# Two bursts per pair instead of five short steps: reordering an attention stream inside a PE-bound kernel

## The chip, the core and the metric

The kernel runs on one core of one Trainium2 chip. The core has a matrix engine (PE, with its weight loads shown apart as PEld), a vector engine (DVE), a scalar engine (ACT), a general engine (POOL) and a queue engine that issues DMAs (SP). Each runs its own instructions strictly in the order in which the program lists them and waits at semaphores for the others. The metric is device time in microseconds (us). All times here are of one execution each; six executions of the kernel before were timed, and one more number, the span, comes from the profiled one.

## The reference, cut to what matters

```python
# q, k, v: (8 batches, 8 heads, 576 positions, 64), float32
scores = scale * q @ k.T
mask   = local (0 <= i-j < 32) for heads 0-3, strided (i >= j, i % 32 == j % 32) for heads 4-7
x      = softmax(where(mask, scores, -1e9)) @ v          # -> (4608 tokens, 512)
h      = x @ w_in                                        # (4608, 2048)
out    = relu(h)**2 @ w_out                              # (4608, 512)
```

## The kernel before

**Two streams on one PE.** The matrix part (MoE) is cut into 9 chunks of 512 tokens. For each chunk `mm1(c, ff)` (L402) makes 128 of the 2,048 hidden columns: four matmuls of 128x512 into one `ph` bank, a relu on ACT (L411, out `r`), and a square on DVE (L412, out `g_sb`). `mm2(c, i)` (L416) is a quarter of one output block: four matmuls of 128x512 (L423); after every fourth, ACT copies the block to `y` and SP writes it out. I call each such call a *group*; there are 288, numbered from 0. From chunk 3 on, `mm1` of chunk c and `mm2` of chunk c-1 alternate; before that they run in blocks (groups 32 to 47 are `mm1` of chunk 1, 48 to 63 `mm2` of chunk 1, 64 to 79 `mm1` of chunk 2).

**Attention is woven in between.** The unit is a pair of heads: pair u = 4 * batch + p, where p = 0, 1 are local and p = 2, 3 strided. After batch 0, which runs by itself ahead of the groups, each pair has these steps:

- T: PE transposes q and k (L233), with a copy on ACT (q) or DVE (k, L248). Only for the earlier batches; later ones have it done by DMA (L150, L162).
- S(u) (`step_S`, L254): 12 (local) or 16 (strided) small matmuls of 64 rows of contraction (L277) into four PSUM tiles `pt`. Four exps follow on ACT (L282) and two mask multiplies on DVE (L288), one for each head. They are not issued at once: the first exp comes with the step; `later(k, ...)` (L292 to L296) defers the second exp by one group, the first mask and the third exp by two, the fourth exp by three and the second mask by four. Each lands behind that group's relu or square in its engine's order.
- D(u, part) (`step_D`, L342): 6, 6 or 4 matmuls (L359) of the exps with v, then a reciprocal and a multiply on DVE (L370, L371), out `x_l` or `x_s`. A local pair has two parts, a strided pair three. Before its matmuls, a D step issues at once whatever of its own pair's deferred work is not issued yet (L343).
- E(u) (`step_E`, L374): the transpose of x into `xt`. Local pairs of batch 2 and later do it by one DMA from SP's queue (L381). Strided pairs use 8 transposes on PE (L388) and a copy (L396), on ACT for u < 12 and on DVE from there.

The scores, the D outputs and the transposes share one pool of five PSUM banks (`ps_t`); `r` has four buffers, `ph` two.

**What sets the order.** `stream_steps` (L459) lists the steps: for each u the order is S(u+1), E(u-1), D(u,0), [T], D(u,1), [T], and D(u,2) for a strided pair. `ends[u-1]` notes the place in this list at which E(u-1) is over. The planner at the end of the kernel then spreads the list over the groups: for each batch b it takes the steps between the last `ends` and `ends[4*b+3]` and assigns them in proportion to group weights, with one count for each step in the list, whatever it holds:

```python
for b in range(1, B):
    g_end, s_end = ready.get(b, starts[b]), ends[4 * b + 3]
    ...
    for g in range(g_prev, g_end + 1):
        due[g] = done_prev + (s_end - done_prev) * sum(weights[g_prev:g]) // total
```

The last E of batch b is thus due exactly ahead of the first `mm1` group that reads batch b: groups 80, 112, 144, 176 and 208 for batches 3 to 7 (batch 1 by group 32, batch 2 by group 56).

Of the kernel before, what the change touches and what calls it, by code (L numbers as in the profile page):

```python
# [14 lines left out]
def kernel(  # L15
# [78 lines left out]
    def is_local(u):  # L94
        return units[u][1] < H // 4
# [118 lines left out]
    def run_due(test):  # L214
        due = [x for x in pending if test(x)]
        for x in due:
            pending.remove(x)
        for x in sorted(due, key=lambda x: x[0]):
            x[2]()
# [5 lines left out]
    def step_T(u, name):  # L225
        s = st[u]
        local = is_local(u)
        n, w = (6, QL) if local else (NJ, SP_)
        src = s[name]
        src = src.rearrange("p j h d -> p (j h d)" if local else "p h c -> p (h c)")  # L230
        pt = ps_t.tile([128, S], BF16, name="pt")
        for j in range(n):
            nc.tensor.transpose(pt[:, w * j:w * (j + 1)], src[:, 128 * j:128 * (j + 1)],  # L233
                                ident[0:w, 0:w])
        if local and name == "k":
            full = kTl[v_slot(u)]
            dst = full[:, 32:32 + S]
        else:
            full = dst = qkT.tile([128, S], BF16, name=f"{name}T")
        if local:  # L240
            o = dst.rearrange("c (p j) -> c p j", j=6)
            i = pt.rearrange("c (j p) -> c p j", j=6)
        else:
            o, i = dst, pt
        if name == "q" and u not in (1, 3):
            nc.scalar.copy(o, i)
        else:
            nc.vector.tensor_copy(o, i)  # L248
        s[name + "T"] = full

    def blk_pos(h, j):
        return NJ * (j % 2) + 4 * h + j // 2
# [89 lines left out]
    def step_D(u, part):  # L342
        run_due(lambda x: x[1] == u)  # L343
        s = st[u]
        e, vt = s["e"], s["v"]
        if is_local(u):
            w, kn, n0, n1, tot = QL, 128, 6 * part, 6 * part + 6, 2 * NL
            rhs = vt.rearrange("p h t d -> p (h t) d")
            pos = lambda n: QL * n
            src = lambda n: n  # L350
        else:
            w, kn, tot = SP_, SP_, NBS
            n0, n1 = ((0, 6), (6, 12), (12, 16))[part]
            rhs = vt
            pos = lambda n: SP_ * blk_pos(n % 2, n // 2)
            src = lambda n: NJ * (n % 2) + n // 2
        po = ps_t.tile([128, 6, D + 1], FP32, name="pt")
        for n in range(n0, n1):
            nc.tensor.matmul(po[:, n - n0, :], e[0:kn, pos(n):pos(n) + 128],  # L359
                             rhs[0:kn, src(n), 0:D + 1], start=True, stop=True)  # L360
        if part == 0:
            s["x"] = x_pool.tile([w, tot, D], BF16, name="x_l" if is_local(u) else "x_s")
        x = s["x"]
        if is_local(u):
            x = x.rearrange("p (t h) d -> p h t d", h=2)[:, part]
        else:
            x = x[:, n0:n1, :]
        m = n1 - n0
        rinv = small.tile([128, 6, 1], FP32, name="rinv")
        nc.vector.reciprocal(rinv[0:w, 0:m], po[0:w, 0:m, D:D + 1])  # L370
        nc.vector.tensor_tensor(x, po[0:w, 0:m, 0:D],  # L371
                                rinv[0:w, 0:m].to_broadcast([w, m, D]), op=ALU.mult)

    def step_E(u):  # L374
        s = st[u]
        b, p = units[u]
        x = s["x"]
        local = is_local(u)
        n, w = (NL, QL) if local else (NJ, SP_)
        if local and b >= XB:  # L380
            nc.sync.dma_start_transpose(  # L381
                out=xt[p][:, b * S:(b + 1) * S].rearrange("c (t q) -> c t q", q=QL),
                in_=x.rearrange("p n d -> p (n d)"))
            st.pop(u)
            return
        px = ps_t.tile([128, S], BF16, name="pt")
        for t in range(n):
            nc.tensor.transpose(px[:, w * t:w * (t + 1)],  # L388
                                x[:, 2 * t:2 * t + 2, :].rearrange("p h d -> p (h d)"),
                                ident[0:w, 0:w])  # L390
        dst = xt[p][:, b * S:(b + 1) * S]
        copy = nc.scalar.copy if u < 12 else nc.vector.tensor_copy
        if local:
            copy(dst, px)
        else:
            copy(dst.rearrange("c (p j) -> c p j", j=NJ),  # L396
                                  px.rearrange("c (j p) -> c p j", j=NJ))
        st.pop(u)
# [32 lines left out]
    T_ = lambda u, nm: (lambda: step_T(u, nm))  # L431
    S_ = lambda u: (lambda: step_S(u))
    D_ = lambda u, part: (lambda: step_D(u, part))
    E_ = lambda u: (lambda: step_E(u))
# [9 lines left out]
    def first_steps():  # L444
        t, n, o = T_, (lambda u: lambda: step_N(u)), (lambda u: lambda: step_O(u))
        order = []
        for i, u in enumerate(first_order):
            order += [t(u, "q"), t(u, "k")]
            if i > 1:
                order.append(n(first_order[i - 2]))  # L450
            order.append(S_(u))
        a, b, c, d = first_order
        order += [n(c), lambda: run_due(lambda x: x[1] == d), o(a), n(d), o(b), o(c), o(d)]
        return [(fn, 0 if i < len(order) - 7 else 6) for i, fn in enumerate(order)]

    def has_T(u):
        return units[u][0] < (LB if is_local(u) else XB)

    def stream_steps(lo, hi, base):  # L459
        order = [T_(lo, "q"), T_(lo, "k"), T_(lo + 1, "q"), S_(lo), T_(lo + 1, "k")]  # L460
        ends = {}
        for u in range(lo, hi + 1):
            if u < hi - 1:
                order.append(S_(u + 1))
            if u > lo:
                order.append(E_(u - 1))
                ends[u - 1] = base + len(order)
            if u < hi:
                order.append(D_(u, 0))
                if u + 2 < hi and has_T(u + 2):  # L470
                    order.append(T_(u + 2, "q"))
                order.append(D_(u, 1))
                if u + 2 < hi and has_T(u + 2):
                    order.append(T_(u + 2, "k"))
                if not is_local(u):
                    order.append(D_(u, 2))
        return order, ends
# [65 lines left out]
    for e in es:  # L543
# [3 lines left out]
                            base=-1, channel_multiplier=1, pattern=[[-1, QL]])  # L547
    nc.gpsimd.affine_select(out=ml, in_=ml, compare_op=ALU.is_ge, fill=0.0,
                            base=32, channel_multiplier=-1, pattern=[[1, QL]])
# [7 lines left out]
                            base=0, channel_multiplier=-1, pattern=[[1, SP_]])  # L557
# [5 lines left out]
    first = first_steps()  # L563
# [9 lines left out]

    NCH = T // 512
    steps, ends = stream_steps(4, 8, 0)
    more, more_ends = stream_steps(8, 4 * B, len(steps))
    steps = steps + more
    ends.update(more_ends)
# [108 lines left out]
```

## Time and profile before

| | |
|---|---|
| six timed executions | median 325.72 us (323.76 to 327.46) |
| the profiled execution | 326.22 us, of which the profiled span is 324.2 us (2.0 us lie around it) |
| matmuls of 128x512 | 1,152 records (L408 576, L423 576), each shown as about 380 ns |
| mean start-to-start of those, within a group of four | 216 ns (for instance 102.442 to 102.658 us, and 103.026 to 103.241) |
| ACT busy, DVE busy | 164.4 us (51%), 168.6 us (52%) |
| granted PE clock | 1.00 in all stretches from 4 us to the end of the span |

The page gives busy time by engine, a row of tenths over the span, the chain that ended last, and groups of instructions with what ended the idle time before them. Matmuls are pipelined, so that their shown durations overlap: a group of four takes 0.86 us from its first start to the next group's first start, though its bar is 1.03 us long. Starts are what is compared below. In a timeline line the columns are start, length, engine, source line, operation, output<-inputs, shape and count; an idle gap ahead of it and what ended that gap follow in brackets.

### The profile page before, as it was taken

How to read it: one execution, taken by the hardware profiler on the slowest of the kernel's cores; microseconds unless marked ns; L12 is line 12 of the kernel's file. 1: busy time of each engine (PE TensorE's matmuls, PEld its weight loads, DVE VectorE, ACT ScalarE, POOL GpSimd, SP SyncE). 2: the span in 40 equal slices, each digit the busy share in tenths (PEclk: the TensorE clock that was granted, in tenths of full speed). 3: DMA queues.
4: the chain of work that ended last, by engine and by line, in shares of the span. 5: the costliest groups of instructions: out<-in, count | busy, mean ns of one | idle time of the engine just before them, and what ended most of it. 6: DMA issues, size and time to landing. Idle time of an engine off the chain costs nothing.

```text
span 324.2 us, 6229 instructions
## 1 busy us (share of the span) xinstructions
PE 304.3 (94%) x2390; PEld 153.1 (47%) x2390; DVE 168.6 (52%) x413; ACT 164.4 (51%) x338; POOL 87.2 (27%) x113
## 2 busy tenths in 40 slices
PE   2699999899989998999999999999999999999995
PEld 1465445444555544444444544454445444444442
DVE  5544555656975786656566656565455222222200
ACT  3662764567745674544554555554554444444411
POOL 8514472573920813722074007000000000000000
PEclk9999999999999999999999999999999999999999
DMA  7999999999999999999499557000110010000021
GB/s 182 182 195 229 208 151 253 195 291 232 214 140 201 208 223 180 216 192 188 111 212 228 137 123 172 34 32 34 51 53 32 32 67 33 32 34 32 32 95 69
DMA packets 87222, 44.81 MB, mean 138 GB/s; under 512 B 71769, under 2 KB 80377, under 8 KB 87001
## 3 DMA queue, kind: packets, MB, share of 16 engines
q1 hardware_dynamic: 77448, 34.81, 49.4%
q0 software_dynamic: 9744, 9.60, 18.6%
q8 instruction: 19, 0.31, 0.4%
q14 instruction: 11, 0.08, 0.1%
HBM read 36.89 MB, written 12.98 MB: 154 GB/s over the span
## 4 chain that ended last, share of the span: by engine, by line
PE 88%; DVE 5%; DMA 2%; ACT 2%; issue 1%; ACTq 0%; POOLq 0%
PE ph L408 38%; PE py L423 27%; PE ph L423 10%; PE pt L277 4%; PE pt L359 4%; DMA qT_s<-in_q_dram 2%; PE pt L233 2%; PE py L440 2%; DVE e L288 1%; DVE xt L396 1%; PE pt L388 1%; DVE x_s L371 1%; PE pt L332 1%; ACT e L282 1%; DVE kTl L248 1%
## 5 line engine op out<-in xcount | busy, mean ns | idle before, releaser
L408 PE MATMUL ph<-xt,w_in_b 128*128 128x512 bf16 x576 | 146.2, 382 | 1.8 <-DVE xt L396 1.7
L411 ACT ACTIVATE r<-ph 128x512 bf16<-128x512 f32 x144 | 86.0, 597 | 104.6 <-PE ph L408 99.5
L412 DVE TENSOR_TENSOR g_sb<-r 128x512 bf16<-128x512 bf16 x144 | 69.0, 480 | 107.1 <-ACT r L411 106.3
L423 PE MATMUL py<-w_out_b,g_sb 128*128 128x512 bf16 x400 | 102.7, 379 | 0.0
L423 PEld LDWEIGHTS <-g_sb 128*128 128x128 bf16 x576 | 52.8, 98 | 59.6 <-issue 3.1
L408 PEld LDWEIGHTS <-w_in_b 128*128 128x128 bf16 x576 | 52.2, 98 | 54.9 <-issue 2.0
L282 ACT ACTIVATE e<-pt 72x288 bf16<-72x288 f32 (+1 forms) x128 | 48.7, 406 | 14.4 <-PE pt L277 14.2
L423 PE MATMUL ph<-w_out_b,g_sb 128*128 128x512 bf16 x176 | 42.4, 379 | 0.0
L181 POOL CAST vl<-vl_st 128x768 bf16<-128x768 f32 x14 | 13.8, 984 | 57.4 <-DMA vl_st<-in_v_dram 41.4
L359 PEld LDWEIGHTS <-e 128*128 128x128 bf16 (+1 forms) x392 | 21.0, 97 | 15.6 <-DVE e L288 0.5
L288 DVE TENSOR_TENSOR e<-e,mask_str 72x576 bf16<-72x576 bf16 x32 | 19.2, 602 | 7.8 <-ACT e L282 7.8
L371 DVE TENSOR_TENSOR x_s<-pt,rinv 72x384 bf16<-72x384 f32 (+1 forms) x42 | 21.4, 509 | 1.4
L122 POOL CAST q_l<-q_st 96x768 bf16<-96x768 f32 x15 | 12.6, 839 | 26.4 <-DMA q_st<-in_q_dram 22.6
L427 ACT COPY y<-py 128x512 f32<-128x512 f32 x25 | 14.6, 585 | 4.0 <-PE py L423 4.0
L122 POOL CAST k_l<-k_st 96x768 bf16<-96x768 f32 x14 | 12.1, 863 | 16.9 <-DMA k_st<-in_k_dram 16.6
L370 DVE RECIPROCAL rinv<-pt 96x6 f32<-96x6 f32 (+2 forms) x70 | 12.9, 184 | 6.5 <-PE pt L359 6.5
L427 ACT COPY y<-ph 128x512 f32<-128x512 f32 x11 | 6.4, 585 | 19.4 <-PE ph L423 19.4
L371 DVE TENSOR_TENSOR x_l<-pt,rinv 96x384 bf16<-96x384 f32 x28 | 15.5, 554 | 1.0
L197 POOL CAST vs<-v_st 72x1024 bf16<-72x1024 f32 x14 | 15.4, 1126 | 0.5 <-DMA v_st<-in_v_dram 0.2
L288 DVE TENSOR_TENSOR e<-e,mask_loc 128x576 bf16<-128x576 bf16 x32 | 14.9, 464 | 1.0 <-ACT e L282 1.0
L359 PE MATMUL pt<-vs,e 72*128 72x65 bf16 x224 | 13.8, 193 | 0.1
L182 POOL CAST vl<-vl_st 32x640 bf16<-32x640 f32 x14 | 11.7, 835 | 0.9
(74 smaller groups left out, 156.2 us busy)
## 6 DMA issues: line engine op xcount, KB each, us to landing
out_dram<-y SPq DMA_DIRECT2D x36, 256.0 KB, 2.0
vl_st<-in_v_dram SPq DMA_DIRECT2D x28, 144.0 KB, 3.6
v_st<-in_v_dram SPq DMA_DIRECT2D x14, 288.0 KB
q_st<-in_q_dram SPq DMA_DIRECT2D x8, 288.0 KB, 7.7
k_st<-in_k_dram SPq DMA_DIRECT2D x8, 288.0 KB, 8.2
q_st<-in_q_dram SPq DMA_DIRECT2D x16, 144.0 KB, 7.9
k_st<-in_k_dram SPq DMA_DIRECT2D x16, 144.0 KB, 6.5
w_in_b<-in_moe_w_in_dram POOLq DMA_DIRECT2D x4, 512.0 KB, 11.2
```

The costliest lines, as they stand in the source:

```text
L122: copy(t.rearrange("p j h d -> p h j d"), s[name + "f"].rearrange("p h (j d) -> p h j d", j=6))
L181: nc.gpsimd.tensor_copy(t[:, :, :, 0:D].rearrange("p h t d -> p (h t) d"), s["vf"])
L197: (copy or nc.gpsimd.tensor_copy)(t[:, :, 0:D], s["vf"].rearrange("p h (j d) -> p (h j) d", d=D))
L282: nc.scalar.activation(e[0:kn, lo:lo + S // 2], banks[row][half][0:kn, 0:S // 2], AF.Exp, scale=scale)
L288: nc.vector.tensor_tensor(x, x, m.to_broadcast([kn, n, w]), op=ALU.mult)
L359: nc.tensor.matmul(po[:, n - n0, :], e[0:kn, pos(n):pos(n) + 128], rhs[0:kn, src(n), 0:D + 1], start=True, stop=True)
L371: nc.vector.tensor_tensor(x, po[0:w, 0:m, 0:D], rinv[0:w, 0:m].to_broadcast([w, m, D]), op=ALU.mult)
L408: nc.tensor.matmul(ph, w_in_b[:, kk, 128 * ff:128 * (ff + 1)], xt[kk][:, 512 * c:512 * (c + 1)], start=(kk == 0), stop=(kk == 3))
L411: nc.scalar.activation(r, ph, AF.Relu)
L412: later(1, lambda: nc.vector.tensor_tensor(g[:, ff, :], r, r, op=ALU.mult))
L423: nc.tensor.matmul(py, g[:, ff, 128 * j:128 * (j + 1)], w_out_b[:, ff, :], start=(ff == 0), stop=(ff == 15))
L427: nc.scalar.copy(y, py)
```

## The change

For u >= 12 (batch 3 on), `stream_steps` puts S(u+1) and E(u-1) into one list entry, and all D parts of pair u into another:

```diff
         for u in range(lo, hi + 1):
+            if u >= 12:
+                first = ([S_(u + 1)] if u < hi - 1 else []) + [E_(u - 1)]
+                order.append(lambda f=first: [fn() for fn in f])
+                ends[u - 1] = base + len(order)
+                if u < hi:
+                    order.append(lambda u=u: [step_D(u, i) for i in range(2 if is_local(u) else 3)])
+                    if u + 2 < hi and has_T(u + 2):
+                        order += [T_(u + 2, "q"), T_(u + 2, "k")]
+                continue
             if u < hi - 1:
                 order.append(S_(u + 1))
```

No instruction is added or dropped, and the order among the attention steps themselves stays S, E, D, D, D. A batch from 3 on has 8 entries in place of 18 (16 in batch 7, where no S of a next batch is left), so that in batches 4 to 7 an entry comes every fourth group. The entry counts also move steps of pairs below 12: S(13) with E(11), at u = 12, is one entry, which makes batch 2's stretch one entry shorter and shifts the proportional assignment there. In the two lists, the group ahead of which each step stands:

| step | before | after |
|---|---|---|
| S(8), S(9) | 37, 40 | 38, 40 |
| D(8,0), D(8,1) | 41, 42 | 41, 43 |
| D(9,0), D(9,1) | 46, 47 | 47, 48 |
| T(12) k, D(10,2), S(12) | 51, 52, 52 | 52, 52, 53 |
| E(10), D(11,0), D(11,1), D(11,2) | 53, 53, 54, 55 | 53, 54, 55, 56 |
| S(13) with E(11) | 56 | 56 |
| D(15,0), D(15,1), D(15,2) | 73, 75, 77 | 76 |
| S(17), E(15) | 79, 80 | 80 |
| D(19,0), D(19,1), D(19,2) | 105, 107, 109 | 108 |
| S(21), E(19) | 111, 112 | 112 |

Batches 5 and 6 repeat the last two lines 32 and 64 groups later.

## The prediction

> **What bounds the kernel now.** I read the page's shares first, then PE's waits, then PE's timeline, because only the last tells what a step costs.
>
> ```profile
> PE 304.3 (94%) x2390; PEld 153.1 (47%) x2390; DVE 168.6 (52%) x413; ACT 164.4 (51%) x338; POOL 87.2 (27%) x113
> PE 88%; DVE 5%; DMA 2%; ACT 2%; issue 1%; ACTq 0%; POOLq 0%
> ```
>
> PE is busy for 94% of the span and is 88% of the chain that ended last; DVE and ACT are half idle. PE's waits, by what ended them (total us, times, longest):
>
> ```profile
> PE pt L277 <- DVE kTl L248: 3.4, 4, 1.0
> ...
> PE ph L408 <- DVE xt L396: 1.7, 5, 0.9
> ...
> PE pt L388 <- DVE x_s L371: 0.7, 2, 0.5
> PE pt L277 <- ACT e L282: 0.5, 1, 0.5
> ...
> PE pt L359 <- DVE e L288: 0.2, 1, 0.2
> ```
>
> What the change can win in waits is little: from 85 us on, the timeline shows 1.03 us at S(12), 0.1 at E(11), 0.90 at E(15) and 0.20 at each of the four later batch ends, 2.8 us in all. The price of a short step is read from starts in PE's timeline, in steady state:
>
> ```profile
> 150.96 1.03 PE L408 MATMUL ph<-xt,w_in_b 128*128 128x512 bf16 x4
> 151.83 0.28 PE L359 MATMUL pt<-vs,e 72*128 72x65 bf16 x4
> 151.95 1.03 PE L423 MATMUL py<-w_out_b,g_sb 128*128 128x512 bf16 x4
> 152.81 1.03 PE L408 MATMUL ph<-xt,w_in_b 128*128 128x512 bf16 x4
> 153.77 0.43 PE L277 MATMUL pt<-kT,kTl 64*128 64x96 bf16 x12
> 154.13 1.04 PE L423 MATMUL py<-w_out_b,g_sb 128*128 128x512 bf16 x4
> 155.01 0.42 PE L388 MATMUL pt<-ident,x_s 72*128 72x72 bf16 x8
> 155.27 0.81 PE L408 MATMUL ph<-xt,w_in_b 128*128 128x512 bf16 x3
> 156.28 0.38 PE L408 MATMUL ph<-xt,w_in_b 128*128 128x512 bf16 x1 [0.20 <-DVE xt L396]
> ```
>
> A group before D takes 0.87 us, as one before another group (0.86): D costs its 0.12 and nothing to enter. Ahead of S the group takes 0.96: 0.1 to enter. E (0.26) enters free. The last line is a batch end: `mm1` waits for E's copy.
>
> **Joining D parts.** Before already has two local parts in one place, D(13):
>
> ```profile
> 102.66 0.53 PE L359 MATMUL pt<-vl,e 128*128 128x65 bf16 x12
> 103.03 1.02 PE L423 MATMUL ph<-w_out_b,g_sb 128*128 128x512 bf16 x4
> ```
>
> 12 matmuls in 0.368 us; 6 alone (106.119 to 106.305) 0.186, after which the group's first gap is 2 ns longer (218 for 216). A join saves about 5 ns. Pairs 12 to 31 have 10 local and 10 strided: 30 joins, 0.15 us. Here a rule of the Trainium skill says otherwise: "TensorE: Matmul & The Clock Gate", Part 3, The mechanism, lets a weight load overlap running matmuls only where it goes to other rows of the array. Both D and `mm1` use the full rows (tile 128*128), so every entry would expose one load, 97 ns by the row of L359. The change removes 3 entries of a strided pair and 1 of a local one, 40 in all: 3.9 us. The trace decides: D's first matmul starts 216 ns after the group's last (102.442 to 102.658), the plain pitch, so the load is hidden. I take 0.15.
>
> **Joining S and E.** Only strided E is on PE, and E(14), (15), (18), (19), (22), (23), (26) and (27) get an S ahead. S's way out into a full-height tile costs 131 ns (last scores matmul 186.182, next load 186.313) whether a group or E follows; alone, it lengthens the group's first gap to 227 ns. About 10 ns saved each, 0.1 us. The one such pair in before, S(13) with E(11), shows the danger: 97.19 for E's load in place of 97.08, since D(11,2)'s multiply ended at 97.14.
>
> **Waits from batch 3 on.** D's burst gives DVE 0.70 + 0.70 + 0.55 = 1.95 us in one piece (a reciprocal's start to the start of what follows its multiply: 116.289 to 116.996 for six matmuls, 91.398 to 91.944 for four). The next entry is four groups, 3.46 us, away, and only `mm1` groups bring squares (0.34 each, 75.646 to 75.989); at a batch end DVE has about 0.2 + 1.95 + 2 x 0.34 = 2.8 us to do by the time E is through, 3.46 + 0.49 + 0.73 = 4.7 after D's start. So the 0.20 us at groups 112, 144, 176 and 208 stay. In the order of the built program no later S or D waits for an exp, mask or multiply issued less than two groups ahead of it; S and E together take all five banks, but their former owners are a burst older. Local E and its DMA keep their place in SP's queue but for one `y` write a batch, which then goes ahead; POOL's list stays; the groups that read those columns come over ten groups later.
>
> E(15) at group 80 changes. Before, E follows the `mm1` of group 79 directly, and its copy stands behind that group's square, which waits for the relu: 122.12 + 0.20 + 0.63 + 0.34 = 123.30, copy to 124.05, wait 0.90. Now S(17) (0.46) stands between, so relu and square run beside it: the copy still starts about 1.2 after group 79, but the `mm1` needs it 0.36 to 0.46 later. DVE, with D(15) at 76 instead of 73 to 77, is done with four squares by then. I take 0.3 gained (bounds: 0.45 gained; 0.5 lost if POOL's casts hold DVE).
>
> **Waits in batch 2, where the counting moves steps.** This is the largest item, and not one that the change names.
>
> ```profile
> 76.80 0.43 PE L277 MATMUL pt<-qT,kTl 64*128 64x96 bf16 x12 [0.70 <-DVE kTl L248]
> 77.16 1.04 PE L408 MATMUL ph<-xt,w_in_b 128*128 128x512 bf16 x4
> 78.03 0.34 PE L359 MATMUL pt<-vl,e 128*128 128x65 bf16 x6
> ...
> 91.53 0.43 PE L277 MATMUL pt<-qT,kTl 64*128 64x96 bf16 x12 [1.03 <-DVE kTl L248]
> ```
>
> S(8) goes from group 37 to 38, D(8,0) stays at 41. With four groups between, the second mask is issued ahead of D; with three, `step_D` issues it itself, and the fourth exp stands behind group 40's relu. D(8,0)'s sixth matmul reads 128 columns from 480, which reach into the second head, so it waits for that mask. From the end of group 40: relu starts +0.21 (73.94 to 74.153), exp +0.49 after it, 0.41 long, mask +0.07, 0.45 long, release 0.04: 1.67 us. The sixth load would be ready at 0.15: **1.52 us of new wait**, with group 41 behind it and everything after. Bounds: 0.16, the only wait of this kind in before (D(4,0), where no relu lay between), to 2.5, if the mask takes 1.43 as one does at 88.69. I take 1.52, since relu and exp are in the path by order. S(9) beside it: S(8)'s own wait of 0.12 for its kTl goes, a wait of 0.17 for S(8)'s third exp is added.
>
> Then DVE regains ground. S(12) now comes a group after T(12)'s k transpose, and PE is 1.5 us later: the 1.03 us at 91.53 goes. S(13) now follows D(11,2), and T(13)'s copy stands behind D(11,1): 0.70 + 0.67 + 0.2 against 0.26 + 0.86 + 0.12 + 0.09 on PE, 0.25 new; E(11) waits 0.22 in place of 0.11. At group 56: 1.52 + 0.05 - 1.03 + 0.25 + 0.11 = **0.9 us behind**.
>
> The second rule bears on the regain. That mask at 88.69 took 1.43 us and not 0.45; two casts of POOL ran from 88.20 to 89.80. "SBUF — State Buffer", section "SBUF: two separate sides", calls the shared port an exclusive lock: the loser is blocked for a whole instruction, and is not slow by itself. By the bare row (1.35 us for this mask wherever it stands) S(12) would still wait 0.15; by the rule the mask, now due at about 90.15 between those casts and the next at 90.43, takes 0.45 and S(12) waits for nothing. I take the rule, and leave 0.15 to the range.
>
> **Sum.** +0.9 - 0.3 - 0.15 - 0.1 = +0.35, say +0.4 on the profiled execution's 326.22 us: 326.6. That execution is 0.5 above the median of the six, so for a median I forecast 325.72 + 0.4 = **326.1 us**. The PE clock is no term: it stayed at 1.00 through 1.03 us waits.
>
> **Rivals.** (1) *Slower: DVE comes late to the batch ends.* Place: E(15), E(19), E(23), E(27), whose copy stands behind D's burst. It decides once DVE is more than 4.7 - 2.8 = 1.9 us later than worked out. For it: casts hold DVE for up to 1 us (above). Against: DVE is 52% busy, and the casts of batches 5 and 6 mostly end before these groups. Price: 0.7 us at each of four ends, 2.8 on the forecast: 328.9. Chance 0.15. (2) *Slower: the regain fails*, S(12) waiting its 1.03 again: 327.2; with a blocked mask at D(8,0), over 327.35. Chance 0.2. (3) *The wait at D(8,0) is not there* (0.16): 326.1 - 1.36 = 324.7. Against: the issue order. Chance 0.1. (4) *Faster: entries do cost*, as the rule on weight loads has it: 326.1 - 3.75 = 322.4. Against: the 216 ns pitch. Chance 0.07. Forecast: 0.48.
>
> 0.5% (1.6 us) is about what a measurement of this kernel can tell from no change. Slower beyond that: (1), half of (2) and a tail of the forecast, 0.28. Faster: (4), a part of (3) and a tail, 0.11. Range 323.9 to 328.9: (1) and (3) inside, (4) left out, with up to 0.6% spread among the six runs.
>
> **What will show it.** In the new trace: D of 12 or 16 matmuls in 0.37 or 0.49 us with no gap ahead; S then E with 131 ns between; about 1.5 us idle at the sixth matmul of D(8,0) near 78 us, ended by DVE's mask; no wait at S(12); some 0.6 us at E(15), 0.2 at the later ends. I am wrong if D(8,0) does not wait, if PE waits for banks or DVE after group 81, or if groups around a burst come nearer than 216 ns pitch allows.

## The result, and the profile after

| | before | after |
|---|---|---|
| executions in one series | 72 | 35 |
| median, lowest to highest (us) | 325.54 (322.53 to 331.02) | 327.24 (323.41 to 332.25) |
| ratio after / before | | 1.0031, 95% interval 1.0010 to 1.0051 |
| profiled execution, its span (us) | 326.22, 324.2 | 330.38, 328.4 |

Slower, by 0.1 to 0.5%: inside what was called no change. The ratio leaves out executions more than 1.5% above the fastest of their kernel, so it lies below the quotient of the medians (1.0052); those executions turn out to be part of the story.

The page of the changed kernel, busy time of the engines and the chain that ended last:

```profile
PE 305.7 (93%) x2390; PEld 153.7 (47%) x2390; DVE 172.7 (53%) x413; ACT 163.9 (50%) x338; POOL 87.2 (27%) x113
PE 85%; DVE 7%; ACT 3%; DMA 2%; issue 1%; SPq 0%; ACTq 0%
```

The instruction counts are the same. DVE gains 4.1 us of busy time with the same 413 instructions, and its part of the chain grows from 5 to 7%: single DVE instructions became longer. The PE waits of the changed kernel (what waits, what ended it, total us, times, longest):

```profile
PE pt L277 <- DVE kTl L248: 2.6, 4, 0.9
...
PE pt L359 <- DVE e L288: 2.1, 2, 2.0
PE pt L277 <- DVE x_l L371: 1.9, 1, 1.9
PE ph L408 <- DVE xt L396: 1.8, 5, 1.0
```

The 1.0 us at S(12) has gone from the first line. Two new waits stand in its place: 2.0 us for a mask in a D step, and 1.9 us of a scores step for a bank that DVE's multiply was to free. Both are in batch 2, whose steps the change does not name. PE's timeline around the first:

```profile
75.69 1.04 PE L408 MATMUL ph<-xt,w_in_b 128*128 128x512 bf16 x4
76.57 0.32 PE L359 MATMUL pt<-vl,e 128*128 128x65 bf16 x5
78.86 0.20 PE L359 MATMUL pt<-vl,e 128*128 128x65 bf16 x1 [1.98 <-DVE e L288]
78.90 3.32 PE L408 MATMUL ph<-xt,w_in_b 128*128 128x512 bf16 x8
82.02 0.54 PE L359 MATMUL pt<-vl,e 128*128 128x65 bf16 x6
```

D(8,0) issues five matmuls and stops at its sixth, as forecast, for 1.98 us. The next line was not forecast: groups 41 and 42 (8 matmuls) need 3.12 us from 78.90 to 82.02 in place of 8 x 0.216 = 1.73. The table by stretches of time (PE, PEld, DVE, ACT and POOL busy, then granted PE clock, DMA share, GB/s) says why:

```profile
75.79:79.20 3.41, 1.43 (x12) 0.71 (x12) 1.77 (x4) 1.34 (x4) 1.11 (x2) 1.00 1.32 219
79.20:82.62 3.42, 3.42 (x15) 1.41 (x14) 1.44 (x4) 1.25 (x3) 2.54 (x4) 0.50 1.08 211
82.62:86.03 3.41, 3.41 (x31) 1.55 (x30) 3.10 (x5) 2.54 (x7) 3.35 (x5) 1.00 1.20 240
```

In the first row PE is idle for 1.98 of 3.41 us. In the second the granted clock is 0.50, so that a matmul takes about twice as long although PE shows 100% busy; in the third it is 1.00 again. (The last section says why the rows are cut at these times.) A little later DVE is busy for all of 6.00 us with only 7 instructions:

```profile
84.00:90.00 6.00, 4.99 (x41) 2.35 (x39) 6.00 (x7) 4.06 (x10) 5.20 (x7) 1.00 1.22 223
```

Three of them, in DVE's timeline:

```profile
84.60 3.15 DVE L412 TENSOR_TENSOR g_sb<-r 128x512 bf16<-128x512 bf16 x2
87.67 1.84 DVE L288 TENSOR_TENSOR e<-e,mask_str 72x576 bf16<-72x576 bf16 x1
```

Two squares in 3.15 us and a mask of 1.84, where undisturbed ones take 0.43 and 0.45. POOL is busy, mostly with casts, for 5.20 of the 6.00 us. PE then meets DVE's backlog at S(11), the second new wait:

```profile
88.63 0.36 PE L277 MATMUL pt<-qT_s,kT_s 64*72 64x72 bf16 x9
90.93 0.33 PE L277 MATMUL pt<-qT_s,kT_s 64*72 64x72 bf16 x7 [1.94 <-DVE x_l L371]
```

To place the loss, take the start of each group in each trace and subtract. Growth against the kernel before, in us, by stretch of groups (the stretch from 40 to 41, for instance, holds group 40 and whatever attention stands between it and group 41). The last two columns are experiments explained below:

| groups | what is in it | before | after | count only | count kept |
|---|---|---|---|---|---|
| 40 to 41 | D(8,0)'s wait | 1.05 | +2.16 | +1.54 | 0.00 |
| 41 to 43 | the slow clock | 1.91 | +1.55 | 0.00 | 0.00 |
| 48 to 49 | S(11)'s wait | 1.36 | +2.15 | +0.13 | 0.00 |
| 49 to 53 | S(12) waits no more, D(11,0) leaves | 6.52 | -1.14 | -0.78 | +0.45 |
| 53 to 56 | D(11,0) comes in, S(13) and E(11) wait | 4.25 | +0.86 | +0.86 | 0.00 |
| **36 to 56** | **batch 2's stretch** | 25.83 | **+5.71** | **+1.75** | **+0.36** |
| 56 to 80 | batch 3 | 24.92 | -0.02 | 0.00 | -0.02 |
| 80 to 81 | E(15)'s wait | 1.93 | +0.11 | +0.57 | -0.47 |
| 81 to 287 | all later batches | 195.14 | -0.08 | 0.00 | -0.08 |

D(11,0) takes 0.18 us and moves from one stretch to the next, so that the waits alone changed by -0.96 and +0.68 there in the changed kernel. The whole loss of the profiled execution lies between groups 36 and 56. That its total grew only by 4.16 us is because its group 36 began 1.50 us earlier than in before's; nothing ahead of it was changed, and this start moves from execution to execution (full clock begins at 30.03 us in before's trace and at 28.00 in the other). The bursts themselves, in batches 3 to 7, are worth 0.1 us.

### The profile page after: what moved, and what is told of

Read it like the earlier page. It is cut to its first block, busy times and chain, and to the rows that moved or that the text cites. A ratio compares the mean times of both kernels' runs of the same rounds, so it can differ in the third digit from the quotient of the medians.

```text
span 328.4 us, 6224 instructions
## 1 busy us (share of the span) xinstructions
PE 305.7 (93%) x2390; PEld 153.7 (47%) x2390; DVE 172.7 (53%) x413; ACT 163.9 (50%) x338; POOL 87.2 (27%) x113
## 4 chain that ended last, share of the span: by engine, by line
PE 85%; DVE 7%; ACT 3%; DMA 2%; issue 1%; SPq 0%; ACTq 0%
PE ph L408 36%; PE py L423 26%; PE ph L423 10%; PE pt L277 4%; PE pt L359 3%; DVE g_sb L412 2%; DMA k_st<-in_k_dram 2%; DVE e L288 2%; PE pt L233 2%; PE py L440 2%; PE pt L388 1%; DVE xt L396 1%; PE pt L332 1%; ACT r L411 1%; ACT e L282 1%
## 5 line engine op out<-in xcount | busy, mean ns | idle before, releaser
L412 DVE TENSOR_TENSOR g_sb<-r 128x512 bf16<-128x512 bf16 x144 | 73.0, 512 | 106.0 <-ACT r L411 105.5
L423 PEld LDWEIGHTS <-g_sb 128*128 128x128 bf16 x576 | 54.4, 98 | 64.3 <-issue 3.2
L408 PEld LDWEIGHTS <-w_in_b 128*128 128x128 bf16 x576 | 53.4, 99 | 58.2 <-issue 2.4
L282 ACT ACTIVATE e<-pt 72x288 bf16<-72x288 f32 (+1 forms) x128 | 47.8, 407 | 10.6 <-PE pt L277 10.4
L181 POOL CAST vl<-vl_st 128x768 bf16<-128x768 f32 x14 | 11.7, 833 | 68.6 <-DMA vl_st<-in_v_dram 44.5
L288 DVE TENSOR_TENSOR e<-e,mask_str 72x576 bf16<-72x576 bf16 x32 | 20.4, 637 | 7.1 <-ACT e L282 7.1
L359 PEld LDWEIGHTS <-e 128*128 128x128 bf16 (+1 forms) x392 | 17.5, 98 | 11.6 <-DVE e L288 2.6
L197 POOL CAST vs<-v_st 72x1024 bf16<-72x1024 f32 x14 | 16.8, 1224 | 1.0 <-DMA v_st<-in_v_dram 0.6
L122 POOL CAST k_l<-k_st 96x768 bf16<-96x768 f32 x14 | 12.8, 912 | 13.1 <-DMA k_st<-in_k_dram 12.6
L359 PE MATMUL pt<-vl,e 128*128 128x65 bf16 x168 | 8.6, 195 | 2.1 <-DVE e L288 2.1
```

Source lines behind the costliest of these rows:

```text
L122: copy(t.rearrange("p j h d -> p h j d"), s[name + "f"].rearrange("p h (j d) -> p h j d", j=6))
L197: (copy or nc.gpsimd.tensor_copy)(t[:, :, 0:D], s["vf"].rearrange("p h (j d) -> p (h j) d", d=D))
L282: nc.scalar.activation(e[0:kn, lo:lo + S // 2], banks[row][half][0:kn, 0:S // 2], AF.Exp, scale=scale)
L288: nc.vector.tensor_tensor(x, x, m.to_broadcast([kn, n, w]), op=ALU.mult)
L408: nc.tensor.matmul(ph, w_in_b[:, kk, 128 * ff:128 * (ff + 1)], xt[kk][:, 512 * c:512 * (c + 1)], start=(kk == 0), stop=(kk == 3))
L412: later(1, lambda: nc.vector.tensor_tensor(g[:, ff, :], r, r, op=ALU.mult))
```

## The experiments

Two theories stood first. **A**: the loss is the shift of batch 2's steps, which comes from the count of list entries, with D(8,0)'s wait as its main part. **B**: the bursts cost time (DVE late behind them, or banks). A third came with the slow clock in the trace. **C**: the wait lowers PE's clock in some executions, and that is most of the price. All ratios are against before on the same chip.

**1. The change with batch 2's count kept.** Only the entry at u = 12 is split, so that every step of batch 2 stands before its old group; all bursts stay.

```diff
-                order.append(lambda f=first: [fn() for fn in f])
+                if u == 12:
+                    order += first
+                else:
+                    order.append(lambda f=first: [fn() for fn in f])
```

> Bursts as in the change from batch 3 on, but S(13) and E(11) stay two list entries, so that every step of batch 2 keeps its group of before (S(8) 37, D(8,0) 41, S(12) 52). Theory 'count' (the loss comes from the shift of batch 2's steps by the shorter list): no wait at D(8,0), the 1.03 us at S(12) is back, group starts from 58 on run parallel to before within 0.3 us, time 0.998 to 1.000 of before. Rival 'bursts' (bursts themselves cost, DVE late to S and E): time about 1.003 of before, lost after group 58.

Measured: 325.39 us median, ratio 1.0003 (0.9969 to 1.0037). The wait at S(12) is back, with 1.51 us; E(15) wins 0.47, more than the 0.3 allowed for. D(8,0) and group 41 in its timeline:

```profile
77.14 0.35 PE L359 MATMUL pt<-vl,e 128*128 128x65 bf16 x6
77.33 1.02 PE L408 MATMUL ph<-xt,w_in_b 128*128 128x512 bf16 x4
```

Six matmuls in one piece, and the group starts 0.19 after the first of them. With the count kept the bursts cost nothing and bring nothing that the interval (0.4% either way) could show: B falls.

**2. The count alone.** The kernel before, with its five short steps, and S(13) with E(11) in one entry.

```diff
+            if u == 12:
+                order.append(lambda u=u: (step_S(u + 1), step_E(u - 1)))
+                ends[u - 1] = base + len(order)
-            if u < hi - 1:
+            elif u < hi - 1:
                 order.append(S_(u + 1))
-            if u > lo:
+            if u > lo and u != 12:
```

> The kernel before with one edit: S(13) and E(11) are one list entry. Nothing else is joined, five steps stay everywhere. Theory 'count': the wait of 1.5 to 2 us at the sixth matmul of D(8,0) appears and the time is 1.002 to 1.004 of before. Rival 'bursts': 1.000 of before.

Measured: 327.35 us, ratio 1.0046 (1.0021 to 1.0072). One merged entry, with no D burst anywhere, costs as much as the whole change:

```profile
75.02 0.32 PE L359 MATMUL pt<-vl,e 128*128 128x65 bf16 x5
76.70 0.20 PE L359 MATMUL pt<-vl,e 128*128 128x65 bf16 x1 [1.36 <-DVE e L288]
```

The profiled execution kept its clock, so it gives the pure shift: the stretch from group 40 to 41 is 1.54 longer. In 7 of 22 executions the mean granted clock was below 0.997.

**3. The changed kernel without the one dependency.** D(8,0)'s sixth matmul reads 96 columns of the exps in place of 128, so that it does not touch the second head's mask; the 32 left out give rows that nothing reads.

```diff
         for n in range(n0, n1):
-            nc.tensor.matmul(po[:, n - n0, :], e[0:kn, pos(n):pos(n) + 128],
+            m_ = w if u == 8 and n == 5 else 128
+            nc.tensor.matmul(po[0:m_, n - n0, :], e[0:kn, pos(n):pos(n) + m_],
```

> The changed kernel, with the sixth matmul of D(8,0) reading its own 96 columns in place of 128, so that it does not reach into the second head and does not wait for the second mask; all steps stay at their groups. Theory 'count, by way of D(8,0)': the 1.98 us wait and the slow groups 41 to 43 after it go; time 0.996 to 1.000 of before. Rival 'DVE backlog' (DVE is late through all of groups 41 to 56 and only the place of the wait changes): the wait turns up at S(10) or S(11) and the time stays near 1.003.

Measured: 324.86 us, ratio 1.0002 (0.9971 to 1.0033), 1 of 14 executions with a lowered clock.

```profile
77.26 0.36 PE L360 MATMUL pt<-vl,e 128*128 128x65 bf16 x6
77.45 1.89 PE L409 MATMUL ph<-xt,w_in_b 128*128 128x512 bf16 x8
```

All else of the shift is in this kernel, and 36 to 56 grows by 0.36 in place of 5.71. The wait at D(8,0), with what it brings, is the loss; the rival, a wait that only moves, falls but for a rest of 0.46 us at S(11).

**4 and 5. The wait filled.** The changed kernel with 30, or 12, matmuls of 128x128 whose result nothing reads (the kernel's own `warm`) ahead of D(8,0)'s sixth. The wait stays; PE is just not idle in it.

```diff
+            if u == 8 and n == 5:
+                warm(30)
             nc.tensor.matmul(po[:, n - n0, :], e[0:kn, pos(n):pos(n) + 128],
```

> The changed kernel, with 30 matmuls of 128x128 on the identity (result unused) ahead of the sixth matmul of D(8,0): PE works through most of the wait. Theory 'clock' (an idle PE of 2 us is granted a lower clock afterwards, and this costs 1.4 us on top of the wait): granted clock 0.999 or more in every execution, groups 41 to 43 at 0.87 us each, time 1.000 to 1.001 of before. Rival 'the wait alone': clock as in the changed kernel or no matter, time about 1.003 of before.

> The changed kernel with 12 dummy matmuls in place of 30 ahead of the sixth matmul of D(8,0): the step ends at the same time, but PE is idle for about 0.9 us of it. Theory 'clock needs a long idle stretch' (1.03 us at S(12) in before left the clock at 1.00): at most 1 in 10 executions under 0.997 mean granted clock, time about 1.0025 of before as with 30. Rival 'any gap at this place': low clock in about 4 of 10 executions as in the changed kernel.

Measured: with 30, 326.16 us, ratio 1.0027 (1.0001 to 1.0053); with 12, 326.80 us, 1.0027 (0.9999 to 1.0056). In none of the 22 executions of either was the clock below 0.997. That was expected; the time expected with 30 (1.000 to 1.001) was missed. The 30 in the timeline:

```profile
77.44 0.32 PE L361 MATMUL pt<-vl,e 128*128 128x65 bf16 x5
77.60 1.84 PE L442 MATMUL py<-ident 128*128 128x128 bf16 x30
79.27 0.19 PE L361 MATMUL pt<-vl,e 128*128 128x65 bf16 x1
79.30 1.89 PE L410 MATMUL ph<-xt,w_in_b 128*128 128x512 bf16 x8
```

And the 12, with what is left of the wait:

```profile
77.69 0.83 PE L442 MATMUL py<-ident 128*128 128x128 bf16 x12
79.22 0.20 PE L361 MATMUL pt<-vl,e 128*128 128x65 bf16 x1 [0.70 <-DVE e L288]
79.25 1.89 PE L410 MATMUL ph<-xt,w_in_b 128*128 128x512 bf16 x8
```

Groups 41 and 42 are back at 1.89 us shown, where they took 3.32. The medians stay above before's of the same series by 0.94 (325.22) and 0.95 (325.85), since the wait is still on the path. With the gap open the change's medians were 1.70 and, in the next experiment, 2.02 above before's. So the fall of the clock is worth about 0.8 to 1.1 us of a median. The ratios, by what they leave out (see the result), cannot tell the filled kernels from the change.

**6. The change once more**, for more executions beside these, and a second profile. No edit.

> The changed kernel itself, for a second profile on the same chip as the runs beside it. Theory: wait of 1.5 to 2 us at D(8,0) in this profile too; groups 36 to 56 take 1.5 to 2 us more than before if the clock holds, up to 6 if it falls; about 4 of 10 executions under 0.997.

Measured: 327.87 us, ratio 1.0019 (0.9989 to 1.0049). Wait and slow groups came again (the clock record has 0.50 from 77.48 to 80.89 us):

```profile
77.92 0.24 PE L359 MATMUL pt<-vl,e 128*128 128x65 bf16 x1 [1.99 <-DVE e L288]
77.97 3.33 PE L408 MATMUL ph<-xt,w_in_b 128*128 128x512 bf16 x8
```

Groups 36 to 56 took 6.82 us more than before, over the 6 allowed for: the clock fell a second time, at 91.13 us, behind waits of 0.82 and 0.70 at S(11) and T(12) (last section).

Executions with a mean granted clock below 0.997 (one stretch of 3.41 us at 0.50 brings the mean of this program to 0.995):

| kernel | gap at D(8,0) | executions at a low clock |
|---|---|---|
| the change (both series) | open | 24 of 58 |
| count only | open | 7 of 22 |
| the change, batch 3's v casts left out (7, below) | open | 5 of 20 |
| filled by 30, by 12 | closed, 0.70 left | 0 of 22, 0 of 22 |
| second mask not needed | none | 1 of 14 |
| count kept | none | 0 of 14 |
| before (three series) | none | 9 of 163 |

In the first series the change's 20 executions at 0.997 or more have a mean of 326.17 us, the 16 others 329.23, which is 3.1 more. In the other three series with an open gap the difference is 2.0 to 2.3. One stretch of 3.41 us at half the clock can cost at most 1.71 (groups 41 to 43 lose 1.55 and 1.43 in two profiles), so these executions were longer for another reason too, longer waits perhaps; that is not shown. C holds in its first part, the wait lowers the clock. As for its price, closing the gap takes away about half of the median's loss, not most of it.

**7. Is S(11)'s wait, behind POOL's casts, a cost of its own?** The changed kernel with POOL's casts of batch 3's v left out.

```diff
         t = vls[v_slot(u)]
+        s["v"] = t
+        if u in (12, 13):
+            return
         nc.gpsimd.tensor_copy(t[:, :, :, 0:D].rearrange("p h t d -> p (h t) d"), s["vf"])
...
         t = vss[v_slot(u)]
+        s["v"] = t
+        if u in (14, 15):
+            return
```

> The changed kernel without POOL's casts of batch 3's v (L181, L182, L197 for pairs 12 to 15; that batch's attention then multiplies an older v). Theory 'POOL holds DVE' (the ground that DVE should regain after D(8,0) is lost because squares and masks of groups 43 to 49 take 1 to 2 us beside these casts): squares there back to 0.43 us, no wait over 0.3 us at S(11), the wait at D(8,0) stays at 1.4 to 2 us; groups 36 to 56 take 0.5 to 1 us more than before if the clock holds. Rival 'DVE is late by its own work': S(11) and T(12) wait as before.

Measured: 327.69 us, ratio 1.0049 (1.0022 to 1.0076): not less than the change. Its DVE timeline at the same place:

```profile
83.99 0.43 DVE L418 TENSOR_TENSOR g_sb<-r 128x512 bf16<-128x512 bf16 x1
85.36 0.43 DVE L418 TENSOR_TENSOR g_sb<-r 128x512 bf16<-128x512 bf16 x1 [0.94 <-ACT r L417]
```

The squares are back at 0.43, and S(11) runs its 16 matmuls in one piece: POOL's casts did stretch them (with v's left out, those of q and k also ran elsewhere: none from 79.3 to 88.8 us). In its trace groups 36 to 56 grow by 3.50 us in place of 5.71. But the times did not follow, so the expectation missed. The wait at D(8,0) is there with 1.99 us, and the profiled execution has the slow groups again (0.50 from 79.21 to 82.62 us). What S(11)'s wait alone is worth remains open.

**8. Earlier transposes at the batch ends.** The traces left one cost in both kernels: at every batch end `mm1` waits for E's copy. Here the kernel of experiment 1 is taken and, at u = 16, 20, ..., 32, E(u-1) becomes an entry ahead of S(u+1), so that the planner puts it some groups before its reader. Two variants beside it: the same with T(12) k and T(13) k ahead of D(10,1) and D(11,1) (9, and once more as 10), and the same early E in the kernel *before*, with its five short steps (11).

```diff
                 if u == 12:
                     order += first
+                elif u % 4 == 0:
+                    order += [first[-1], first[0] if u < hi else (lambda: None)]
                 else:
```

> A version meant to beat both: x1_keep_count, with E of each batch's last pair as an entry of its own ahead of S, so that its copy is done some three groups before the mm1 that reads it. Expected: the waits of 0.20 us at groups 112, 144, 176, 208 and of 0.4 to 0.9 at group 80 go, 1.2 to 1.7 us less than before in the trace from group 56 on, time 0.994 to 0.998 of before. If DVE is late in these stretches, the waits only move and it stays at 1.000.

> y1_early_E with the k transposes of T(12) and T(13) ahead of D(10,1) and D(11,1) in place of after them, so that their copies are earlier in DVE's order. Expected: up to 0.7 us of S(12)'s 1.03 us wait goes, 0.992 to 0.998 of before; if D(10,2)'s multiply then holds up E(10), nothing is won over y1.

> y2_early_E_T again, for more executions: 0.987 to 0.992 of before.

> The kernel before, five steps kept, with E of each batch's last pair ahead of S from batch 3 on and a group or two earlier. Theory 'the early E is what wins, not the bursts': 0.990 to 0.995 of before, the waits at groups 80, 112, 144, 176 and 208 gone. Rival 'bursts are needed for it': 0.998 or more.

| kernel | median us | ratio (95%) | executions |
|---|---|---|---|
| 8: bursts, count kept, early E | 322.64 | 0.9901 (0.9871 to 0.9931) | 22 |
| 9: with early T | 322.41 | 0.9892 (0.9843 to 0.9942) | 6 |
| 10: 9 once more | 323.25 | 0.9916 (0.9887 to 0.9945) | 14 |
| 11: five short steps, early E | 321.95 | 0.9929 (0.9902 to 0.9956) | 16 |

All four beat before, 8 and 9 by more than was expected. The one without a single burst (11) gains about as much as the others, and bursts without the early E (experiment 1) gain nothing, so the gain belongs to E's place ahead of S; a further gain from the early T can't be seen. A batch end of the eleventh, in PE's timeline:

```profile
182.15 0.42 PE L388 MATMUL pt<-ident,x_s 72*128 72x72 bf16 x8
182.41 1.03 PE L423 MATMUL py<-w_out_b,g_sb 128*128 128x512 bf16 x4
183.37 0.43 PE L277 MATMUL pt<-kT,kTl 64*128 64x96 bf16 x12
183.73 1.04 PE L408 MATMUL ph<-xt,w_in_b 128*128 128x512 bf16 x4
```

A group and S lie between the transposes and the `mm1` that reads them, and no wait is left. (At the last of the five batch ends, with one group between, the eleventh still loses some 0.2 us.) In the eighth kernel's trace the stretch from group 80 to 81 is 1.06 shorter than in before, and 81 to 287 is 1.51 shorter, 2.6 us in all; 1.2 to 1.7 was expected, for the reason given in the next section.

## Why the prediction was right, and where its terms were off

The forecast was 326.1 us with "no change" the likeliest; 327.24 was measured. The mechanism was the right one in its main part: the bursts are free, and the time is lost in batch 2, at D(8,0), by the count of entries (experiments 1 to 3). That the median missed by no more than 1.1 us is partly luck: the regain, E(15) and the clock all turned out slower than forecast, and the range of 5 us was wide enough for that. By its steps:

- **Joining D, S and E**: 0.25 us forecast over all pairs, 0.08 measured over batches 4 to 7, where about 0.18 of it was due. Far from 3.9: entries do not expose a weight load. So the rule on weight loads and array rows, as it was read, lost against the trace, and rival 4 falls. (The same section of the skill also lets a load run ahead into the array's background weight buffer, which the prediction left out; no run here tells which it is.) A later pair in the changed kernel, with its batch end; the first four lines are those of batch 3:

```profile
125.95 0.43 PE L277 MATMUL pt<-kT,kTl 64*128 64x96 bf16 x12
126.31 0.43 PE L388 MATMUL pt<-ident,x_s 72*128 72x72 bf16 x8
126.58 0.81 PE L408 MATMUL ph<-xt,w_in_b 128*128 128x512 bf16 x3
128.40 0.38 PE L408 MATMUL ph<-xt,w_in_b 128*128 128x512 bf16 x1 [1.01 <-DVE xt L396]
...
187.05 0.65 PE L359 MATMUL pt<-vs,e 72*128 72x65 bf16 x16
187.54 1.03 PE L408 MATMUL ph<-xt,w_in_b 128*128 128x512 bf16 x4
...
192.73 0.38 PE L408 MATMUL ph<-xt,w_in_b 128*128 128x512 bf16 x1 [0.20 <-DVE xt L396]
```

- **D's burst and DVE**: 16 matmuls take 0.49 us from start to start with no gap, and the later batch ends keep their 0.20, all as forecast. Rival 1 (DVE late to the ends) did not come.
- **E(15)**: 0.3 gained was forecast; the profile shows 1.01 us of wait for 0.90, and the stretch is 0.11 longer. In the first experiment the same burst gains 0.47. The bounds (0.45 gained, 0.5 lost) held, the value did not; it depends on where POOL's casts happen to fall beside the squares. In the changed kernel four squares stood behind D's burst, the last two stretched to 0.90 and 1.00 us beside casts that run from 125.24 to 128.37; in the first experiment no cast fell there and each took 0.43 or less:

```profile
125.01 2.67 DVE L412 TENSOR_TENSOR g_sb<-r 128x512 bf16<-128x512 bf16 x4
```

- **The wait at D(8,0)**: 1.52 forecast, 1.54 measured in the second experiment; the path (relu, exp, mask by the order of issue) was right. In the two profiles of the change itself it was 2.16 and 2.17 by starts, since a square (1.04 us, first profile) or the mask (1.08, second) was held while POOL cast beside it; that lies within the bound of 2.5.
- **The regain**: 0.9 behind at group 56 was forecast, 1.75 in the count-only trace. From group 49 to 56 the forecast has -1.03 + 0.25 + 0.11 = -0.67, and that trace +0.08. S(12)'s wait did vanish, but only 0.60 was gained around it there (0.96 in the change), and S(13) and E(11) cost 0.68 where 0.36 was put. S(11)'s wait (0.13 there, up to 2.15 in the change) no term held. Executions that kept the clock were on the mean 0.4 us above before's mean in the first series and 0.9 to 1.5 in the three others with an open gap, so the 0.4 of the sum was too small for most.
- **The mask between two casts**: S(11)'s first mask, for which the exclusive lock was used, ran at 93.14 us in the change and took 0.45, after the casts had ended at 89.20. In the count-only trace it ran at 87.28 beside casts and took 1.55. S(12) waited in neither. So the 0.45 came about by delay and not by the gap.
- **"The PE clock is no term: it stayed at 1.00 through 1.03 us waits."** This is the step that failed. A wait of 1.52 to 2.5 had just been worked out, longer than the 1.03 that was the proof, so the clock's answer to it was an extrapolation and should have had a term. The clock fell in 36 of 100 executions with the gap open, and closing the gap took 0.8 to 1.1 us off the median: about the 1.1 by which the forecast missed.
- **Rivals 2 and 3**: rival 2 came in part. The regain did fail and DVE was held up at D(8,0), as it said, but S(12), its place, does not wait; its 327.2 was nearly met by way of the clock, which it did not reckon with. Rival 3, no wait at D(8,0), is the third experiment and not the change.

The batch ends teach a second point on size. The forecast priced them by the shown idle, 0.20 us. By starts, group 112 to 113 takes 1.23 with the wait and 0.87 without: 0.36. A 128x512 matmul is shown 379 ns long but is followed at a pitch of 216, so idle is counted from an end that is 0.16 us late.

## What to carry to other kernels

Where a planner spreads list entries in proportion, merging two of them moves steps that the edit does not mention; compare the placement of every step before costing the edit. Price a wait by start-to-start times, add up the idle time that stands close together (here within 3.4 us), ask whether it is more than any the profile has shown the PE clock to survive, and shorten or fill it if it is. And look at who reads a transpose: five E steps put one to three groups ahead of their readers gained 0.7 to 1%, while joining steps that the queue already ran back to back gained nothing.

## What the hardware showed that was not expected

**The clock falls by windows of 3.41 us.** In the change's two profiles and in experiment 7's, every fall before the last matmul lasts 3.41 us at 0.50, and in the profile with two they begin 13.65 us apart, four times 3.41. So time can be cut into windows of 3.41 us on each trace's own grid. The first profile of the change around S(11):

```profile
86.03:89.44 3.41, 2.96 (x32) 1.47 (x30) 3.41 (x4) 2.51 (x6) 3.17 (x4) 1.00 1.16 205
89.44:92.86 3.42, 1.93 (x25) 1.29 (x26) 3.14 (x11) 0.50 (x2) 0.00 (x0) 1.00 1.01 141
92.86:96.27 3.41, 3.39 (x40) 1.75 (x38) 2.77 (x8) 1.85 (x5) 1.05 (x1) 1.00 0.84 103
```

The second, behind S(11) and T(12):

```profile
87.72:91.12 3.40, 1.89 (x31) 1.17 (x25) 3.30 (x9) 0.81 (x2) 2.92 (x4) 1.00 1.25 235
91.13:94.54 3.41, 3.41 (x17) 1.42 (x14) 1.44 (x4) 0.94 (x2) 0.77 (x1) 0.50 1.31 139
```

| wait | PE idle in the window | clock in the next |
|---|---|---|
| D(8,0), the change, first profile | 1.98 | 0.50 |
| D(8,0), experiment 7 | 1.99 | 0.50 |
| D(8,0), the change, second profile | 1.70 | 0.50 |
| S(11) and T(12), the same | 1.51 | 0.50 |
| S(11), the change, first profile | 1.49 | 1.00 |
| D(8,0), count only | 1.37 | 1.00 |
| S(12), experiment 1 | 1.35 | 1.00 |

The 1.94 us at S(11) lay across two windows, 0.45 in one and 1.49 in the next, and the clock stayed; two short waits of 0.82 and 0.70 in one window lowered it. In these traces, then, idle time within a window tells the falls from the others better than the length of a wait, with the border near 1.5 us. It is not the whole rule: in the second profile a window that holds the last matmuls of the program, with 1.93 idle, still left 1.00 behind it. Where the windows fall differs from execution to execution, and so does the wait (1.36 to 1.99 us in four profiles). Either would make the fall a matter of chance, as in 36 of 100 executions; how much each does is not shown. The Trainium skill ("TensorE: Matmul & The Clock Gate", Part 1, What's actually happening) has a free-running window of about 3.4 us, and the 3.41 agrees; but it puts the fall after an idle window, and here 1.5 to 2 us of idle in one were enough, so there the measurement decides. At the start of before's trace the view's 1.00 is no reading, as the clock record begins at 30.03 us: until then `mm1`'s matmuls start 427 ns apart, and 216 from there on.

**DVE beside POOL's casts.** Squares of 0.43 us and masks of 0.45 became 0.9 to 2.2 us while POOL cast v, q or k, and squares were 0.43 again where no cast ran (experiment 7). That agrees with the exclusive lock that the prediction took from the Trainium skill ("SBUF — State Buffer", SBUF: two separate sides). Casts that follow each other closely hold one instruction more than once: the mask of 1.84 us stood beside two, from 87.41 to 89.20.
